# A long convolution by two-stage transforms: radix 64 first and radix 32 second, with real and imaginary parts on partitions

## The chip, the core and the metric

The kernel runs on one core of a Trainium2 chip. The metric is the time of one execution on the device, in microseconds (us). A core has a matrix engine (TensorE, written PE in the profile, with its weight loads listed apart as PEld), a vector engine (DVE), a scalar engine (ACT), a general engine (POOL, GpSimd) and a queue engine (SP) that mostly issues DMAs. TensorE reads its operands from SBUF and writes to PSUM; DVE and ACT read PSUM and write SBUF. A matmul may use only a part of the 128 x 128 array: the profile writes such a tile as rows x columns, so that 64*32 means 64 rows of contraction and 32 output partitions. Tiles in different places of the array can work at the same time.

## The reference

A layer norm feeds two branches, whose product is added to the input:

```python
xn = layernorm(x)                       # x: 2048 x 512
K  = einsum("dn,dnl,dn->dl", C, exp(dt*A*l), dt*B).real      # 512 x 2048 kernel, N = 128 states
y  = irfft(rfft(pad(xn.T)) * rfft(pad(K)))[:, :2048].T + xn * Dskip
g  = silu(gelu(xn @ w1 + b1) @ w2 + b2) # w1: 512 x 1792, w2: 1792 x 512
out = x + y * g
```

The convolution is causal, of length 2048, for each of 512 channels. The output must agree in float32.

## The kernel before

**Front.** A written order of steps (the string `ORDER`, lines 48 to 128) interleaves four kinds of work: the layer norm, the two dense products of the feed-forward branch (each value split into a high and a low part of type fp32r, so three products for one, lines 256 to 258 and 295 to 297), the parameters of the scan, and the generation of the kernel K (functions `gen_...`). K leaves for DRAM in `gen_keep` (line 666, tile `ko`). The kernel `K` for a group of channels comes from small matmuls of 128*32 with 64 columns of moving data (line 656).

**Scan.** The convolution is a product of length-2048 transforms with shifted frequencies (k + 1/4), so that no padding is needed. Channels are worked in four blocks `b` of 128 channels. A transform is done in two stages, 2048 = 32 x 64 before the change:

- `first_dft` (line 856) does the radix-32 stage for the signal (`u` = 0) and for the kernel (`u` = 1). The data of a block are the stationary operand, the small table `fc` is the moving one: 32*128 tiles, four row groups, 64 moving columns. `first_out` copies PSUM to the tile `X`, on ACT, and for block 0 on ACT and DVE.
- `second_dft` (line 874) does the radix-64 stage with twiddles folded into the table `mc`: 64*64 tiles, 128 moving columns, and real and imaginary parts added up in PSUM (the loop over `c`). There are eight groups `g` of frequencies in a block.
- `spectrum` (copy of the signal's spectrum by ACT, `uh`), `product` (two DVE products per group, tiles `t`) and `combine` (DVE, tile `Y`, four instructions of 64 partitions for two groups) multiply the two spectra.
- `back_dft` (line 914) is the first inverse stage: one full 128*128 matmul for a frequency, 128 moving columns; `back_out` copies to `Z`.
- `swing` transposes `Z` on TensorE, `swing_out` copies to `bs`, `last_dft` (line 969) does the last stage in 64*32 tiles with 512 moving columns (for part of the last block `rows_out`, line 1006, in 128*64 tiles), and `last_out` multiplies by the gate and adds the input (`gb`, `xb`), after which `store` writes to DRAM.

**Order.** In both parts the instructions of an engine run in the order of the program text; a framework adds the semaphore waits. `slot(b, g)` (line 1020) is one step of the scan: the second stage of group `g` of block `b`, beside it the first stage of block `b+1`, and the inverse stages of the same or the block before. After the front come four `first_dft` calls of block 0, mixed with the last products of the feed-forward branch (line 1105), and then 32 slots and a tail (lines 1125 to 1144).

**PSUM and DMA.** `bank` (line 804) gives out the one-bank PSUM tiles of the scan in turn from two tags of two; the second stage has its own two-bank tiles (`ri`, two of them). DMA issues of the scan wait in the queue of SP in program order: tables (`mc`, `tcn`), the raw signal (`raw`, from `xs`), the kernel (`in`, from `kgd`), gate and input for the tail (`gb`, `xb`), and the stores. `dsk` holds the skip weights, added to tap zero of the kernel by POOL in `side_skip` (line 851); it is filled in the front (`skip_load`, line 729).

All matmuls of the scan are of type float32, and the profile lists two weight loads and two matmuls for each call of such a matmul: for example 1,024 calls of line 883 (32 in each of 32 slots) stand as 2,048 in the profile. A transpose (line 936) stands as one.

Of the kernel before, what the change touches and what calls it, by code (L numbers as in the profile page):

```python
# [20 lines left out]
P = 128  # L21
# [4 lines left out]
N1, N2 = 32, 64  # L26
NB = 4
# [103 lines left out]
def _shape_constants():  # L131
    n1 = np.arange(N1)[:, None]
    k1 = np.arange(N1)[None, :]
    a = 2 * np.pi * n1 * (k1 + 0.25) / N1
    cf = np.tile(np.stack([np.cos(a), -np.sin(a)], 1), (G, 1, 1))
    cg = np.zeros((2, N1, 2, 3, N1))
    for hh in range(2):
        for c, v in enumerate((np.cos(a).T, -np.sin(a).T)):
            cg[hh, :, c, 0] = v
            cg[hh, :, c, 1:].reshape(N1, N1, 2)[:, :, hh] = v  # L140
    cg = cg.reshape(P, 3 * N1)
    n2 = np.arange(N2)[:, None]
    k2 = np.arange(N2)[None, :]
    cm = np.zeros((2, N2, N1, 3, N2))
    ct = np.zeros((2, N2, N1, 2, N2))
    for k in range(N1):
        th = 2 * np.pi * (n2 * (k + 0.25) / L + n2 * k2 / N2)
        c, s = np.cos(th), np.sin(th)
        cm[:, :, k, 0, :] = c
        cm[:, :, k, 1, :] = s  # L150
        cm[:, :, k, 2, :] = -s
        ct[0, :, k, 0, :] = c.T / L
        ct[1, :, k, 0, :] = -s.T / L
        ct[0, :, k, 1, :] = s.T / L
        ct[1, :, k, 1, :] = c.T / L
    ct = ct.reshape(P, N1, 2, 2, 2, 16).transpose(0, 1, 4, 5, 3, 2)
# [6 lines left out]
    return {  # L163
        "cf": cf.reshape(P, 2 * N1).astype(f),
        "cg": cg.astype(f),
        "cm": cm.reshape(P, N1 * 3 * N2).astype(f),
        "ct": ct.reshape(P, N1 * P).astype(f),
        "cb": cb.reshape(CH * NPC, CH * NPH).astype(ml_dtypes.bfloat16),
    }
# [3 lines left out]
def kernel(  # L173
# [7 lines left out]
    x_t = u[0].rearrange("(n h j t a q) d -> t h a j n q d", n=N1, h=2, j=2, t=2, a=2)  # L181
    o_l = out[0].rearrange("(r j q) d -> j r q d", j=2, q=NQ)
    o_t = out[0].rearrange("(n h j t a q) d -> t h a j n q d", n=N1, h=2, j=2, t=2, a=2)
# [20 lines left out]
    dsk = keep.tile([P, NB, DB], F32, name="dsk")  # L204
    GP.memset(dsk, 0.0)
    b1s = keep.tile([P, NF], F32, name="b1s")
    fc = keep.tile([P, 2 * N1], F32, name="fc")
# [452 lines left out]
    def gen_out(s):  # L660
        gen[s]["ko"] = ko = par.tile([P, DD, N2], F32, tag="ko", name=f"ko{s}", bufs=2)
        A.copy(ko, gen[s]["p"])

    def gen_keep(s):
        b, j = divmod(s, SPB)
        SY.dma_start(kgd[b][:, j * DD * N2:(j + 1) * DD * N2], gen.pop(s)["ko"].rearrange("p a b -> p (a b)"))
# [62 lines left out]
    def skip_load():  # L729
        for g in range(G):  # L730
            SY.dma_start(dsk[g * N1:g * N1 + 1], dskip.rearrange("(o b g d) -> g o b d", o=1, b=NB, g=G)[g])
        SY.dma_start(fc, cf)
# [50 lines left out]
    def open_front():  # L783
        SB["pf"] = pf = opened(p2, "pf", "right")
        SB["mc"] = pf.tile([P, N1, 3, N2], F32, name="mc")
        SB["psa"] = opened(p2, "psa", "right", bufs=2, space=PSUM)

    def open_mid():
        SB["pm"] = pm = opened(p2, "pm", "right")
        SB["ps"] = opened(pz, "psm", "left", bufs=2, space=PSUM)  # L790
        SB["tcn"] = pm.tile([P, N1, P], F32, name="tcn")
        SB["gc"] = pm.tile([P, N1], F32, name="gc")

    def table_load(t, src):
        w = t.shape[2] if len(t.shape) == 3 else t.shape[2] * t.shape[3]
        for k in range(0, N1, 8):
            d = t[:, k:k + 8]
            SY.dma_start(d.rearrange("p k m -> p (k m)") if len(t.shape) == 3 else d.rearrange("p k a m -> p (k a m)"),
                         src[:, k * w:(k + 8) * w])
# [13 lines left out]
    def stage_close():  # L813
        sg.close()
        SB["raw1"] = opened(fa, "raw", "left").tile([P, N2, DB], F32, name="raw1")

    def side_piece(b, g):
        t = side.setdefault(b, SB.get("raw1"))
        SY.dma_start(t[g * N1:(g + 1) * N1], xs.rearrange("(n m) (b g d) -> b g n m d", n=N1, b=NB, g=G)[b, g])

    def side_load(b):
        if b:
            t = SB["pf"].tile([P, N2, DB], F32, tag="in", name=f"raw{b}", bufs=2)
        else:
            t = wka.tile([P, N2, DB], F32, tag="xh", name="raw0", bufs=2)
# [4 lines left out]
    def side_turn(b):  # L830
        if b:
            t = SB["pf"].tile([P, DB, N2], F32, tag="in", name=f"in0_{b}", bufs=2)
        else:
            t = wka.tile([P, DB, N2], F32, tag="xl", name="in0_0", bufs=2)
        raw = side[b].rearrange("p m d -> p d m")
        side[b] = [[t[:, :DB // 2], t[:, DB // 2:]]]
        for h in range(2):
            d, r = side[b][0][h], raw[:, h * DB // 2:(h + 1) * DB // 2]
            GP.tensor_copy(d, r) if b else A.copy(d, r)

    def kernel_load(b):
        if b:
            k = SB["pf"].tile([P, DB, N2], F32, tag="in", name=f"in1_{b}", bufs=2)
            k = [k[:, :DB // 2], k[:, DB // 2:]]
        else:
            k = [wka.tile([P, DB // 2, N2], F32, tag="x", name=f"in1_0_{h}", bufs=2) for h in range(2)]
        for h in range(2):
            SY.dma_start(k[h], kgd[b].rearrange("p (h d m) -> p h d m", h=2, m=N2)[:, h])
        side[b].append(k)

    def side_skip(b):
        for h in range(2):
            k0 = side[b][1][h][:, :, 0]
            GP.tensor_add(k0, k0, dsk[:, b, h * DB // 2:(h + 1) * DB // 2])

    def first_dft(b, u, h, gs):
        if b not in xf:
            xf[b] = SB["pf" if b % 2 == 0 else "pm"].tile([P, 2, 2, N1, N2], F32, tag=f"X{b % 2}", name=f"X{b}")
        src = side[b][u][h]
        ps = [bank(f"s1_{b}_{u}_{h}_{g}").rearrange("p e (i m) -> p (e i) m", m=N2) for g in gs]  # L860
        for i in range(8):
            for g, p in zip(gs, ps):
                r = slice(g * N1, (g + 1) * N1)
                PE.matmul(p[:, i, :], src[r, 2 * i:2 * i + 2, :], fc[r], start=True, stop=True, skip_group_check=True)  # L864
        fp[b, u, h] = list(zip(gs, ps))

    def first_out(b, u, h, engs=(A, A, A, A)):
        for n, (g, p) in enumerate(fp.pop((b, u, h))):
            d, p = xf[b][:, :, u, :, 16 * g + 8 * h:16 * g + 8 * h + 8], p.rearrange("p i (c k) -> p c k i", c=2)
            A.copy(d, p) if engs[n] is A else engs[n].tensor_copy(d, p)  # L870
# [3 lines left out]
    def second_dft(b, g):  # L874
        mc = SB["mc"]
        p = SB["ps"].tile([P, 2, 2, 2, 2, N2], F32, tag="ri", name=f"s2_{b}_{g}", bufs=2)
        for jj in range(2):
            for o in range(2):
                for c in range(2):
                    for ka in range(2):  # L880
                        for r in range(2):
                            k, h = 4 * g + 2 * jj + ka, slice(r * 64, (r + 1) * 64)
                            PE.matmul(p[ka * 64:(ka + 1) * 64, r, o, :, jj], mc[h, k, ((0, 2), (1, 0))[c][o], :],  # L883
                                      xf[b][h, c, :, k, :], start=(c == 0), stop=(c == 1), skip_group_check=True)
        sp[b, g] = p

    def spectrum(b, g):
# [4 lines left out]
        if g % 2 == 0:  # L892
            sm[b, g // 2] = [pm.tile([P, 2, 2, 4, N2], F32, tag=f"t{i}", name=f"t{i}_{b}_{g}", bufs=2) for i in range(2)]
# [8 lines left out]
    def combine(b, j, c, eng, js=slice(0, 4)):  # L902
        t, w = sm[b, j]
        if (b, j) not in yy:
            yy[b, j] = SB["pm"].tile([P, 4, 2, P], F32, tag="Y", name=f"Y_{b}_{j}", bufs=2)
        Y = yy[b, j].rearrange("p j a (r x) -> p a r j x", r=2)
        for ka in range(2):
            r = slice(ka * 64, ka * 64 + 64)
            if c == 0:
                eng.tensor_sub(Y[0:64, ka, :, js], t[r, 0, :, js], w[r, 1, :, js])  # L910
            else:
                eng.tensor_add(Y[64:128, ka, :, js], t[r, 1, :, js], w[r, 0, :, js])

    def back_dft(b, j, h):
        Y = yy[b, j].rearrange("p j a m -> p (j a) m")
        p = bank(f"sa{b}_{j}_{h}")
        for e in range(4):
            PE.matmul(p[:, e, :], Y[:, 4 * h + e, :], SB["tcn"][:, 8 * j + 4 * h + e, :], start=True, stop=True)  # L918
        yy[b, j, h] = p

    def back_out(b, j, h, engs=(A,)):
        if (b, "Z") not in yy:
            yy[b, "Z"] = SB["pm"].tile([P, 32, 2, N1, 2], F32, tag="Z", name=f"Z{b}", bufs=2)
        k = 8 * j + 4 * h
        src = yy.pop((b, j, h)).rearrange("p k (x h c) -> p x h k c", h=2, c=2)
        dst = yy[b, "Z"][:, :, :, k:k + 4, :]
        w = 4 // len(engs)
        for i, eng in enumerate(engs):
            n = slice(w * i, w * i + w)
            eng.copy(dst[:, :, :, n], src[:, :, :, n]) if eng is A else eng.tensor_copy(dst[:, :, :, n], src[:, :, :, n])  # L930

    def swing(b, q4, jj, wide=None):
# [242 lines left out]
```

## Time and profile before

| what | value |
|---|---|
| three runs | 565.67, 566.75 and 886.81 us, median 566.75 us |
| profiled execution, first to last instruction (span) | 564.4 us |
| TensorE matmuls | 7,179 instructions, busy 543.8 us (96%) |
| DVE, ACT, POOL busy | 457.0, 411.5, 297.6 us |
| first `first_dft` in full | 395.39 us |
| first slot | 411.22 us |
| last matmul ends | about 557.3 us |

The page lists no time of its own for the profiled execution beside its span; the span is 2.35 us below the median of the runs, and 1.3 us below the fastest of them. All sums are made against the span. The busy time of TensorE counts a stretch in which any matmul is in flight, so two tiles at work together count once. A line of a timeline gives the start, the length, the engine, the line of the program, and how many instructions of one kind follow each other (x64); in square brackets stands how long the engine stood idle before it and what ended the wait. "issue" there means that nothing the profile shows was waited for.

### The profile page before, as it was taken

The numbers are of one execution on the slowest core, as the hardware profiler recorded it, in microseconds if no ns is written. First come the engines' busy times: TensorE is split into PE (matmuls) and PEld (weight loads), VectorE is DVE, ScalarE is ACT, GpSimd is POOL, SyncE is SP. The second block draws the span as 40 slices with busy tenths as digits, with TensorE's granted clock in tenths as the row PEclk, the third lists the DMA queues.
The fourth block names the chain that finished last, engine by engine and source line by source line (L and its number), as shares of the span: only waits on it lengthen the run. The fifth ranks groups of instructions, "written<-read, shape, count | busy, mean of one in ns | idle before, by whom it ended". The sixth has DMA issues, their size and how long they took to land.

```text
span 564.4 us, 17131 instructions
## 1 busy us (share of the span) xinstructions
PE 543.8 (96%) x7179; PEld 434.5 (77%) x7179; DVE 457.0 (81%) x699; ACT 411.5 (73%) x605; POOL 297.6 (53%) x403
## 2 busy tenths in 40 slices
PE   8898999999999999999999999999999999999995
PEld 8666777777777777777777777777779998988873
DVE  6999999999899789998897976886357656867874
ACT  3587998799977998777998787897355565564542
POOL 4648378449976679969743684370320305114323
PEclk9999999999999999999999999999999999999998
DMA  8967636845192364752258138313978583625945
GB/s 188 281 193 207 186 93 201 240 141 195 54 337 74 107 193 136 257 149 58 44 186 236 52 92 107 110 38 126 362 292 78 132 135 83 174 68 126 207 109 112
DMA packets 108344, 86.91 MB, mean 154 GB/s; under 512 B 44294, under 2 KB 87562, under 8 KB 108268
## 3 DMA queue, kind: packets, MB, share of 16 engines
q1 hardware_dynamic: 97584, 65.37, 44.3%
q0 software_dynamic: 9568, 19.93, 12.0%
q8 instruction: 56, 0.92, 0.7%
q10 hardware_dynamic: 1116, 0.53, 0.4%
q14 instruction: 20, 0.16, 0.1%
HBM read 52.25 MB, written 33.55 MB: 152 GB/s over the span
## 4 chain that ended last, share of the span: by engine, by line
PE 60%; DVE 17%; issue 8%; DMA 7%; ACT 3%; SPq 3%; POOL 2%; POOLq 0%; DVEq 0%; ACTq 0%
PE z L295 8%; PE z L296 7%; PE z L297 7%; PE f L256 7%; PE f L258 7%; PE f L257 6%; PE kg L656 5%; PE s L883 4%; PE s L864 3%; PE ph L595 2%; PE sa L918 2%; DVE ra L609 2%; DVE hl L282 2%; DMA xb<-in_A_u_dram 2%; DMA gb<-gd 1%
## 5 line engine op out<-in xcount | busy, mean ns | idle before, releaser
L618 POOL TENSOR_TENSOR mm<-mm,rc 128x32 f32<-128x32 f32 (+4 forms) x150 | 115.8, 772 | 11.8
L295 PE MATMUL z<-w2h,hh 128*128 128x512 f32 x224 | 97.9, 437 | 0.0
L256 PE MATMUL f<-xh,w1h 128*128 128x512 f32 x220 | 91.4, 415 | 0.1
L297 PE MATMUL z<-w2h,hl 128*128 128x512 f32 x224 | 88.5, 395 | 0.3 <-DVE hl L282 0.3
L296 PE MATMUL z<-w2l,hh 128*128 128x512 f32 x224 | 88.6, 395 | 0.0
L258 PE MATMUL f<-xh,w1l 128*128 128x512 f32 x220 | 87.0, 395 | 1.5 <-DVE w1l L241 1.5
L257 PE MATMUL f<-xl,w1h 128*128 128x512 f32 x220 | 86.7, 394 | 0.0
L883 PE MATMUL s<-X,mc 64*64 64x128 f32 x2048 | 63.8, 272 | 1.4 <-issue 1.4
L900 DVE TENSOR_TENSOR t<-s,uh 128x512 f32<-128x512 f32 x64 | 41.0, 685 | 26.6 <-ACT uh L891 26.3
L883 PEld LDWEIGHTS s<-X,mc 64*64 64x64 f32 x2048 | 56.1, 133 | 5.6 <-issue 3.3
L615 POOL COPY mm<-rc 128x32 f32<-128x32 f32 x30 | 14.1, 469 | 81.5 <-DVE e L648 48.9
L282 DVE TENSOR_TENSOR hl<-hf,hh 128x512 fp32r<-128x512 f32 x56 | 49.9, 894 | 5.6 <-ACT hh L276 5.6
L609 DVE SCALAR_TENSOR_TENSOR ra<-ra,ph 128x512 f32<-128x512 f32 x64 | 43.6, 681 | 8.9 <-ACT ra L603 7.9
L258 PEld LDWEIGHTS f<-xh,w1l 128*128 128x128 f32 x220 | 41.3, 188 | 12.3 <-DVE w1l L241 2.4
L270 ACT ACTIVATE hf<-f,b1s 128x512 f32<-128x512 f32 x56 | 38.2, 688 | 17.1 <-DVE hl L282 9.8
L297 PEld LDWEIGHTS z<-w2h,hl 128*128 128x128 f32 x224 | 42.1, 188 | 11.1 <-DVE hl L282 1.2
L295 PEld LDWEIGHTS z<-w2h,hh 128*128 128x128 f32 x224 | 42.5, 190 | 10.5 <-issue 1.0
L256 PEld LDWEIGHTS f<-xh,w1h 128*128 128x128 f32 x220 | 41.5, 189 | 9.8 <-ACT w1h L239 0.3
L296 PEld LDWEIGHTS z<-w2l,hh 128*128 128x128 f32 x224 | 42.3, 189 | 8.2 <-DVE w2l L241 0.2
L257 PEld LDWEIGHTS f<-xl,w1h 128*128 128x128 f32 x220 | 41.4, 188 | 9.0
L641 DVE TENSOR_TENSOR e<-mm,ra 128x1024 f32<-128x1024 f32 x32 | 42.9, 1340 | 5.8 <-ACT ra L629 3.3
L870 ACT COPY X<-s 128x512 f32<-128x512 f32 x56 | 28.9, 598 | 25.3 <-PE s L864 20.2
(185 smaller groups left out, 1163.6 us busy)
## 6 DMA issues: line engine op xcount, KB each, us to landing
x<-in_A_u_dram SPq DMA_DIRECT2D x16, 256.0 KB
xs<-x SPq DMA_DIRECT2D x16, 256.0 KB
xt_h<-xh POOLq DMA_DIRECT2D x4, 1024.0 KB, 5.4
xt_l<-xl POOLq DMA_DIRECT2D x4, 1024.0 KB, 7.4
kgd<-ko SPq DMA_DIRECT2D x32, 128.0 KB
za<-zo SPq DMA_DIRECT2D x4, 1024.0 KB
xh<-xt_h POOLq DMA_DIRECT2D x4, 1024.0 KB, 6.7
xl<-xt_l POOLq DMA_DIRECT2D x4, 1024.0 KB, 10.1
```

The source lines that it names most:

```text
L256: PE.matmul(p, wh[:, k, :], xh[:, k, :], start=(k == 0), stop=False)
L257: PE.matmul(p, wh[:, k, :], xl[:, k, :], start=False, stop=False)
L258: PE.matmul(p, wl[:, k, :], xh[:, k, :], start=False, stop=(k == KD - 1))
L282: V.tensor_sub(hl, hf, hh)
L295: PE.matmul(z, hh[:, s], wh, start=(f0 == 0 and not rows), stop=False)
L296: PE.matmul(z, hh[:, s], wl, start=False, stop=False)
L297: PE.matmul(z, hl[:, s], wh, start=False, stop=(f0 == FA - 1))
L609: V.scalar_tensor_tensor(ra[:, 0, c], ra[:, 1, c], MAGIC, p, op0=ALU.subtract, op1=ALU.subtract)
L618: GP.tensor_mul(mv[:, :, 0:3:2, w:2 * w], mv[:, :, 0:3:2, 0:w], rc[:, 2 + 2 * i:4 + 2 * i, :].rearrange("p j c -> p c j").unsqueeze(3).to_ ...
L641: V.tensor_mul(e1, m1.unsqueeze(1).to_broadcast([P, 2, CH, N1]), ra[:, :, :, :N1])
L883: PE.matmul(p[ka * 64:(ka + 1) * 64, r, o, :, jj], mc[h, k, ((0, 2), (1, 0))[c][o], :], xf[b][h, c, :, k, :], start=(c == 0), stop=(c == 1 ...
L900: V.tensor_mul(t, p[:, i, :, 1].unsqueeze(1).to_broadcast([P, 2, 2, P]), uh)
```

## The change

The two radices change places: 2048 = 64 x 32 forward, the radix-64 stage first. The tables change with them, and the loops are cut so that a matmul of the three transform stages uses one of eight tiles of the array.

- `first_dft`: 64 rows of contraction, 32 output partitions (64*32), 64 moving columns; the four column groups are real and imaginary part of two channels, the two row groups are two halves of the channels. A block is worked in eight calls of 64 matmuls instead of four calls of 32. The real and the imaginary part of `X` now lie on partitions beside each other.
- `second_dft`: one matmul with 64 rows (real and imaginary part together) replaces two that were added up in PSUM; 32 output partitions, 128 moving columns, 32 matmuls in a slot as before.
- `combine`: two DVE instructions of 128 partitions for two groups instead of four of 64.
- `back_dft`: 32 rows, 64 output partitions, 64 moving columns, two matmuls added up for each result, 128 matmuls in a call and two calls for a block, instead of 32 full matmuls for a block. It fills four banks at once. `back_out` copies two banks on ACT and two on DVE.
- `last_dft`: two 128*64 matmuls with 512 columns for a quarter block, instead of eight 64*32 for half a block; `rows_out` is gone, since all quarters now leave as rows.
- `slot` gets a new order, the same for all blocks; `gen_out` and `gen_keep` write K in two halves; `side_piece` reads 256 bytes at a time instead of 128; `kernel_load` issues eight DMAs instead of two; `mc` and `tcn` shrink (3.1 to 2.1 MB, 2.1 to 1.0 MB); `dsk` moves into the scan's own pool, and is filled after the front; the tag `in` has three buffers instead of two; `Y` has three.

```diff
-    def first_dft(b, u, h, gs):
+    def first_dft(b, i):
+        u, h, n = i // 4, i // 2 % 2, i % 2
...
-        ps = [bank(f"s1_{b}_{u}_{h}_{g}").rearrange("p e (i m) -> p (e i) m", m=N2) for g in gs]
-        for i in range(8):
-            for g, p in zip(gs, ps):
-                r = slice(g * N1, (g + 1) * N1)
-                PE.matmul(p[:, i, :], src[r, 2 * i:2 * i + 2, :], fc[r], start=True, stop=True, skip_group_check=True)
+        ps = [bank(f"s1_{b}_{i}_{e}").rearrange("p a (c k) -> p (a c) k", k=M1) for e in range(2)]
+        for x in range(8):
+            for rc in range(4):
+                for e in range(2):
+                    rows, q = slice(e * M1, (e + 1) * M1), slice(rc * 32, (rc + 1) * 32)
+                    PE.matmul(ps[e][q, x, :], src[rows, 16 * n + 2 * x + rc // 2, :], fc[rows, rc % 2, :],
+                              start=True, stop=True, skip_group_check=True)
...
     def second_dft(b, g):
...
         for jj in range(2):
             for o in range(2):
-                for c in range(2):
-                    for ka in range(2):
-                        for r in range(2):
-                            k, h = 4 * g + 2 * jj + ka, slice(r * 64, (r + 1) * 64)
-                            PE.matmul(p[ka * 64:(ka + 1) * 64, r, o, :, jj], mc[h, k, ((0, 2), (1, 0))[c][o], :],
-                                      xf[b][h, c, :, k, :], start=(c == 0), stop=(c == 1), skip_group_check=True)
+                for q in range(4):
+                    for r in range(2):
+                        k, h = 8 * g + 4 * jj + q, slice(r * 64, (r + 1) * 64)
+                        PE.matmul(p[q * 32:(q + 1) * 32, r, o, :, jj], mc[h, k, o, :], xf[b][h, :, k, :],
+                                  start=True, stop=True, skip_group_check=True)
...
-    def combine(b, j, c, eng, js=slice(0, 4)):
+    def combine(b, j, eng, js=slice(0, 4)):
...
+        eng.tensor_sub(Y[:, 0, :, js], t[:, 0, :, js], w[:, 1, :, js])
+        eng.tensor_add(Y[:, 1, :, js], t[:, 1, :, js], w[:, 0, :, js])
...
-        for e in range(4):
-            PE.matmul(p[:, e, :], Y[:, 4 * h + e, :], SB["tcn"][:, 8 * j + 4 * h + e, :], start=True, stop=True)
+    def back_dft(b, lo, hi):
+        ps = [bank(f"sa{b}_{lo}_{q}").rearrange("p a (j m) -> p (a j) m", m=2 * M2) for q in range(4)]
+        for j in range(lo, hi):
+            Y = yy[b, j // 4]
+            for c in range(2):
+                for q in range(4):
+                    for r in range(2):
+                        k, m = slice(q * 32, (q + 1) * 32), slice(r * 64, (r + 1) * 64)
+                        PE.matmul(ps[q][m, j - lo, :], Y[k, j % 4, c, m], SB["tcn"][k, j, c, :],
+                                  start=(c == 0), stop=(c == 1), skip_group_check=True)
...
     def last_dft(b, t):
-        py = [bank(f"y{b}_{t}_{h}") for h in range(2)]
-        for a in range(2):
+        py = bank(f"y{b}_{t}")
+        for jj in range(2):
+            PE.matmul(py[64 * jj:64 * jj + 64], SB["gc"], yy[b, t, "s"][:, jj], start=True, stop=True, skip_group_check=True)
...
+    def slot(b, g):
...
+        if b and g in (3, 4, 6, 7):
+            last_dft(b - 1, (3, 4, 6, 7).index(g))
+        if b and g == 1:
+            back_dft(b - 1, 8, 16)
+        if g == 5:
+            back_dft(b, 0, 8)
+        sw = (2, 3, 4, 6).index(g) if b and g in (2, 3, 4, 6) else None
+        if sw is not None:
             for jj in range(2):
+                swing(b - 1, sw, jj)
+        second_dft(b, g)
+        if nxt:
+            first_dft(b + 1, g)
+        if b and g == 1:
+            back_out(b - 1, 8, 16, (A, V, A, V))
+        if g == 5:
+            back_out(b, 0, 8, (A, V, A, V))
...
+        SB["dsk"] = dsk = pf.tile([P, NB, HB], F32, name="dsk")
+        GP.memset(dsk, 0.0)
+        for e in range(2):
+            SY.dma_start(dsk[e * M1:e * M1 + 1], dskip.rearrange("(o b e d) -> e o b d", o=1, b=NB, e=2)[e])
```

More of the change, by code (lines that the diff above doesn't have):

```diff
@@ new lines, in wide_bank @@
+    def wide_bank(b, t):
+        return SB["ps"].tile([P, 2, 4, P], F32, tag="ri", name=f"w{b}_{t}", bufs=2)
+    def slot(b, g):
+        nxt, last = b + 1 < NB, b == NB - 1
+        if last and g == 0:
+            big = SB["pf"].tile([P, 2, 32, P], F32, tag="X0", name="last")
+            for t in range(4):
+                gx[b, t, "t"] = (big[:, 0, 4 * t:4 * t + 4], big[:, 1, 4 * t:4 * t + 4])
+        if b and g in (3, 4, 6, 7):
[6 more added lines that the diff above has]
+        if sw is not None:
+            for jj in range(2):
+                swing(b - 1, sw, jj)
[6 more added lines that the diff above has]
+            back_out(b, 0, 8, (A, V, A, V))
+        if sw is not None:
+            for jj in range(2):
+                swing_out(b - 1, sw, jj, A)
+        spectrum(b, g)
+        if nxt:
+            first_out(b + 1, g)
+        if b and g in (3, 4, 6, 7):
+            last_out(b - 1, (3, 4, 6, 7).index(g))
+        product(b, g)
+        if g % 2:
+            combine(b, g // 2, V)
+        if b and g in (0, 1, 2, 5):
+            tail_load(b - 1, (0, 1, 2, 5).index(g))
```

365 lines of the change are left out of this document (126 added, 239 removed).

## The prediction

> **What bounds the kernel now.** First the page's shares, then the scan by stretches, then the timeline of TensorE.
>
> ```profile
> span 564.4 us, 17131 instructions
> PE 543.8 (96%) x7179; PEld 434.5 (77%) x7179; DVE 457.0 (81%) x699; ACT 411.5 (73%) x605; POOL 297.6 (53%) x403
> q8 instruction: 56, 0.92, 0.7%
> ```
>
> ```profile
> 395.30:557.30 162.00, 157.15 (x3599) 136.82 (x3599) 107.32 (x162) 85.78 (x155) 43.65 (x50) 1.00 0.64 157
> 440.00:500.00 60.00, 60.00 (x1496) 54.53 (x1488) 40.86 (x60) 35.66 (x66) 12.98 (x12) 1.00 0.60 135
> ```
>
> Columns are busy us and instructions of PE, PEld, DVE, ACT and POOL, then granted clock, DMA share and GB/s. From the first full `first_dft` to the last matmul are 162.0 us, and in 60 us amid the slots PE is busy throughout at full clock, with DVE at 68% and ACT at 59%. The matmuls set the pace, so their groups come next:
>
> ```profile
> L883 PE MATMUL s<-X,mc 64*64 64x128 f32 x2048 | 63.8, 272 | 1.4 <-issue 1.4
> L656 PE MATMUL kg<-e,e 128*32 128x64 f32 x2048 | 35.2, 220 | 0.0
> L864 PE MATMUL s<-fc,in 32*128 32x64 f32 x1024 | 33.8, 273 | 1.1 <-ACT X L870 1.1
> L918 PE MATMUL sa<-tcn,Y 128*128 128x128 f32 x256 | 33.4, 282 | 1.8 <-DVE Y L910 1.8
> L975 PE MATMUL y<-bs,gc 64*32 64x512 f32 x112 | 8.8, 601 | 0.0
> ```
>
> One wait here belongs to no engine: 1.4 us of "issue" before L883. The timeline of PE shows it:
>
> ```profile
> 413.52 0.44 PE L883 MATMUL s<-X,mc 64*64 64x128 f32 x6 [0.34 <-issue]
> 413.89 2.01 PE L864 MATMUL s<-fc,in 32*128 32x64 f32 x64
> 415.84 1.96 PE L883 MATMUL s<-X,mc 64*64 64x128 f32 x58
> 418.72 2.19 PE L883 MATMUL s<-X,mc 64*64 64x128 f32 x70 [0.93 <-issue]
> ...
> 430.52 1.32 PE L883 MATMUL s<-X,mc 64*64 64x128 f32 x39
> 432.00 0.97 PE L883 MATMUL s<-X,mc 64*64 64x128 f32 x25 [0.17 <-issue]
> ```
>
> PE stops in the midst of a run of 64 matmuls, with no one to wait for, and between two stops stand 6 + 64 + 58 = 128 matmuls, each with its weight load (a pair). The q8 row explains the number: 0.92 MB in 56 packets is 16.4 KB a packet, and 0.92 MB over the 2 x 7,179 instructions of TensorE is 64 bytes each, so a packet carries 256 instructions, **128 pairs**. It is TensorE's program, and PE stood because the next packet was not there. The DMA view of four stretches, each with its instruction row if it has one, tells when the packets went:
>
> ```profile
> q1 hardware_dynamic: 348, 1.12, 101.1%
> q1 hardware_dynamic: 128, 0.14, 35.0%
> q8 instruction: 1, 0.02, 6.1%
> q0 software_dynamic: 116, 0.36, 84.3%
> q8 instruction: 1, 0.02, 5.7%
> ```
>
> The first row is 413.5 to 416.3 us: other queues fill the 16 engines and no instruction packet moves. The second and third are 416.3 to 417.4: the packet. PE resumes at 418.72, 2.4 us after the packet began. The fourth is 418.7 to 420.0, again without one, and the fifth 420.0 to 421.1, the next packet. So the following packet is asked for only when PE has entered the one before it: 1.3 us to its start, 2.4 us from there to use. **A turn is 1.3 + 2.4 = 3.7 us for 128 pairs**, and was 418.72 - 413.52 = 5.2 us while tables were loading. Today this mostly hides: at L883's 63.8 / 2,048 = 31 ns a pair, 128 pairs take 4.0 us.
>
> **The change, part by part.** *Work in the array.* How long does one pass take with eight tiles? The timeline of PE shows two shapes at work, and the chain of waits (start, us, what) the segments of a slot and the last block's L1009:
>
> ```profile
> 465.72 1.09 PE L975 MATMUL y<-bs,gc 64*32 64x512 f32 x16
> 466.74 2.05 PE L918 MATMUL sa<-tcn,Y 128*128 128x128 f32 x16
> ...
> 392.76 1.10 PE L656 MATMUL kg<-e,e 128*32 128x64 f32 x64
> 393.80 0.50 PE L295 MATMUL z<-w2h,hh 128*128 128x512 f32 x1
> ```
>
> ```profile
> 422.85 1.91 PE s L883 x64
> 424.76 1.98 PE sa L918 x16
> 426.74 1.91 PE s L883 x64
> 428.65 1.94 PE s L864 x64
> ...
> 555.91 1.06 PE y L1009 x4
> ```
>
> L975 has eight tiles at once: 16 matmuls of 512 columns in 466.74 - 465.72 = 1.02 us, two passes. L656 (four tiles, 64 columns) does 64 in 393.80 - 392.76 = 1.04 us, 16 passes of 0.06. L883 (four tiles, 128 columns) does 16 passes in 1.91: 0.11 each, and 0.17 for the change of tile shape. If eight tiles overlap as four do:
> - `second_dft`: 64 in 8 passes of 0.11 + 0.17 for the change of shape = 1.05 against 1.91; 32 slots: -27.5 us.
> - `first_dft`: 128 in 16 passes of 0.06 + 0.15 = 1.05, eight times a block instead of 1.94 four times: 33.6 against 31.0: +2.6 us.
> - `back_dft`: 256 in 32 passes of 0.06 + 0.1 = 2.0, twice a block, against four of 1.98 (x16): -15.8 us.
> - `last_dft`: 16 of 1.06 (the L1009 row) against seven of 1.02 and two of 1.06: +7.7 us.
>
> Sum **-33 us** in the array. The transposes stay.
>
> *Instructions.* By calls, two pairs each: `first_dft` 2,048 calls instead of 512, so 1,024 pairs become 4,096; `second_dft` stays at 2,048; `back_dft` 1,024 calls instead of 128, 256 pairs become 2,048; the last stage 120 become 64. Added: 3,072 + 1,792 - 56 = **4,808 pairs**, 37.6 packets. The window from 395.3 to 557.3 holds 3,599 today; it will hold 8,407, or **65.7 packets**, and 128 pairs take 0.9 us (first, back) to 1.9 us (second) of array time. Less than a turn, everywhere: PE will wait at nearly every packet boundary.
>
> The price of a turn is not seen in a sustained run, so it is bounded: 2.4 us (no delay to the start) and 5.2 us (the loaded turn). I take 3.6, beside the 3.7 that the rows give, since that start had another queue at 84% next to it. Three turns at the start, under the table loads, take 5.2. Sum: 65.7 x 3.6 + 3 x 1.6 = 241.3 us against 162.0: **+79 us**. The ends: 65.7 x 2.4 = 158 (-4 us) and 65.7 x 5.2 = 342 (+180 us). The array's gain of 33 us is then no gain at all, being inside the waits.
>
> [...]
>
> *Other edits, at nothing.* They hide behind PE, which now waits more:
>
> ```profile
> L910 DVE TENSOR_TENSOR Y<-t,t 64x512 f32<-64x512 f32 x30 | 20.6, 685 | 0.7
> L912 DVE TENSOR_TENSOR Y<-t,t 64x512 f32<-64x512 f32 x30 | 24.0, 799 | 0.7
> L930 ACT COPY Z<-sa 128x512 f32<-128x512 f32 x31 | 18.2, 586 | 16.9 <-PE sa L918 16.9
> L854 POOL TENSOR_TENSOR in<-in,dsk 128x16 f32<-128x16 f32 x8 | 2.0, 249 | 37.5 <-DMA in<-kgd 37.5
> ```
>
> `combine` halves, -22 us of DVE; 16 of the `Z` copies move to DVE, +11; and ACT has 9 less (16 x 586 ns); both engines have 30% and more free in the window above, and without PE's cover both would still have less to do than today. Tables load 2 MB less. `kernel_load` adds 24 DMA issues on SP, the tails drop more (three loads and two stores a quarter instead of six and four). The new `dsk` memset (POOL) and its two DMAs stand in SP's queue ahead of `mc` and behind the release of the front's memory; SP would hold back `mc`, wanted by the first slot, and the kernel, wanted by the third of four first-stage calls. The first-stage calls now take eight packets, some 35 us instead of 16, which covers it; without cover a us or two. The larger `kgd` piece count costs at most the same. The tail after the last matmul keeps its 7 us.
>
> **The rivals.**
> - *The program arrives in time* (chance 0.10). Then the array sets the pace: 564.4 - 33 = 531, about **533 us**, faster. It decides at a turn below 162.0 / 65.7 = 2.47 us on average, and holds wholly below about 1.8, the array time of 128 pairs of the second stage. For it: the 60 us without an idle moment. Against: they need only 12 packets, one in 5 us, and the way from a packet's start to its use is 2.4 us already.
> - *A turn of just 2.4 us* (0.04): 562 us, within 2%.
> - *Eight tiles with 64 columns run no faster than four* (0.04): the change would not do what it says. Then 8,192 pairs at 1.04 / 64 = 16.3 ns are 133 us against 61.1 + 31.0 + 31.7 = 123.8, with `last_dft` +17 us, **584 us**. L975 speaks against it, but at 512 columns. [...]
>
> **How the numbers follow.** The likeliest is the packet-bound scan, 0.82: span 564.4 + 79.3 = 643.7, and 2.35 us more to the median as before (566.75 - 564.4), **646 us**. The average turn could be 2.9 us (a start delay half of the one seen) to 4.3 (every second or third one loaded): 65.7 x 2.9 = 191 gives +33 with the loaded turns, 600 us; 65.7 x 4.3 = 283 gives +125, 692 us. That range leaves out the two cases at the bottom, the 584 of the third, and a little at each end: 0.2 in all. Faster by over 2% 0.10, within 2% 0.04, slower 0.86; 2% is about what a measurement of this kernel can tell from no change.
>
> **What would show it.** In the changed profile: some 93 or 94 packets in the q8 row and 11,987 matmuls; idle time of PE put down to "issue", in stops every 128 pairs, with 3.4 to 3.8 us from one resumption to the next; bursts of eight matmuls of 64 columns in about 0.06 us; DVE's `Y` group near 22 us; the clock perhaps below 1.00, since PE works only a third of the time, which a turn still covers at half speed. Wrong would be a scan with PE busy all through, packets less than 2.4 us apart, or waits at semaphores (`Z`, `X`, the four banks of `back_dft`) longer than a turn, which would add to it.

## The result and the profile after

The changed kernel takes **695.26 us** (median of four runs, 689.54 to 696.67) against 566.21 us before (one of its four runs, a disturbed one of 886.81 us, is left out of the comparison). The ratio is 1.2238, with a 95% interval from 1.2148 to 1.2328: 22% slower. The prediction was 646 us with a range of 600 to 692, so the direction and most of the loss were foreseen, but the measured time lies 3 us above the range.

From the page of the changed kernel; the two rows of digits are slices of a fortieth of the span, with the busy tenths of TensorE and the granted clock in tenths:

```profile
span 694.4 us, 26653 instructions
...
PE 579.8 (83%) x11987; PEld 448.7 (65%) x11987; DVE 441.5 (64%) x678; ACT 405.0 (58%) x589; POOL 294.9 (42%) x397
...
PE   7889999999999999999999865555586767774876
...
PEclk9999999999999999999999989776577858675778
...
q8 instruction: 94, 1.54, 1.0%
```

There are 11,987 matmuls and 94 packets of program, exactly the forecast's counts. Up to the scan little has changed (it begins 1.5 us earlier); in the scan TensorE is busy 50 to 80% instead of throughout, and its clock falls. The scan by stretches (busy us and instructions of PE, PEld, DVE, ACT, POOL, then granted clock, DMA share, GB/s), the first row from the first `first_dft` to the last matmul, the second over 64 whole turns of the program:

```profile
393.80:687.30 293.50, 194.00 (x8405) 152.29 (x8405) 91.08 (x140) 79.03 (x139) 41.57 (x44) 0.74 0.36 82
395.50:676.00 280.50, 182.03 (x8169) 144.03 (x8169) 87.02 (x134) 74.58 (x131) 39.12 (x42) 0.74 0.36 83
```

Before, the same work took 162.0 us with PE busy 157.15 at a clock of 1.00. Now it takes 293.5 us, of which PE has nothing in flight for 99.5. DVE and ACT are busy less than a third of the time, so neither sets the pace. What PE waited for (total us, number of waits, longest):

```profile
PE s L860 <- issue: 51.4, 27, 5.1
PE sa L915 <- issue: 31.9, 15, 4.8
PE s L880 <- issue: 8.2, 9, 2.0
PE s L880 <- ACT X L868: 3.5, 3, 1.2
PE sa L915 <- ACT X L868: 2.2, 8, 0.4
```

91.5 us stand before the three stages of small tiles as "issue", with nobody to wait for; the largest wait for another engine is 3.5 us. The timeline of PE shows the program arriving in blocks:

```profile
566.06 2.25 PE L915 MATMUL sa<-tcn,Y 32*64 32x64 f32 x128 [1.33 <-issue]
569.53 1.47 PE L915 MATMUL sa<-tcn,Y 32*64 32x64 f32 x70 [1.22 <-issue]
570.93 2.50 PE L880 MATMUL s<-X,mc 64*32 64x128 f32 x61
573.02 0.45 PE L860 MATMUL s<-fc,in 64*32 64x64 f32 x10
573.22 0.43 PE L880 MATMUL s<-X,mc 64*32 64x128 f32 x3
573.24 2.02 PE L860 MATMUL s<-fc,in 64*32 64x64 f32 x112
576.75 0.31 PE L860 MATMUL s<-fc,in 64*32 64x64 f32 x6 [1.49 <-issue]
```

PE resumes at 566.06, does exactly 128 pairs and stops; it resumes at 569.53 and does 70 + 61 + 10 + 3 + 112 = 256, two packets, before the next stop. The turns last 3.47 us, and 7.22 us for two. The DMA view of 567.1 to 568.4 has the packet for 569.53:

```profile
q8 instruction: 1, 0.02, 4.9%
```

In the stretch before it, 566.1 to 567.1, no instruction packet moves. So the packet starts only after PE has entered the one before; by the records of the 64 turns each does, 0.03 to 5.89 us after. For this one, 1.1 us pass to its start, 1.0 us for the packet itself and 1.3 us more to its first use, close to the 1.3 and 2.4 us read off before the change.

### The profile page after: what moved, and what is told of

Its sections match the earlier page's. It is cut to its first block, busy times and chain, and to the rows that moved or that the text cites. A ratio compares the mean times of both kernels' runs of the same rounds, so it can differ in the third digit from the quotient of the medians.

```text
span 694.4 us, 26653 instructions
## 1 busy us (share of the span) xinstructions
PE 579.8 (83%) x11987; PEld 448.7 (65%) x11987; DVE 441.5 (64%) x678; ACT 405.0 (58%) x589; POOL 294.9 (42%) x397
## 3 DMA queue, kind: packets, MB, share of 16 engines
q8 instruction: 94, 1.54, 1.0%
## 5 line engine op out<-in xcount | busy, mean ns | idle before, releaser
L860 PE MATMUL s<-fc,in 64*32 64x64 f32 x4096 | 63.2, 253 | 51.4 <-issue 51.4
L860 PEld LDWEIGHTS s<-fc,in 64*32 64x32 f32 x4096 | 54.7, 119 | 59.4 <-issue 59.0
L971 POOL TENSOR_TENSOR xb<-gb,xb 128x512 f32<-128x512 f32 x12 | 15.3, 1276 | 178.9 <-DVE gb L970 178.9
L868 ACT COPY X<-s 128x512 f32<-128x512 f32 x56 | 30.5, 588 | 93.1 <-PE s L860 85.9
L915 PE MATMUL sa<-tcn,Y 32*64 32x64 f32 x2048 | 39.8, 295 | 35.8 <-issue 31.9
L880 PE MATMUL s<-X,mc 64*32 64x128 f32 x2048 | 53.2, 336 | 11.9 <-issue 8.2
L915 PEld LDWEIGHTS sa<-tcn,Y 32*64 32x64 f32 x2048 | 33.7, 181 | 41.9 <-issue 35.4
L926 DVE COPY Z<-sa 128x512 f32<-128x512 f32 x16 | 10.3, 686 | 76.5 <-PE sa L915 76.5
L880 PEld LDWEIGHTS s<-X,mc 64*32 64x32 f32 x2048 | 38.6, 128 | 22.2 <-issue 16.4
```

The source lines that it names most:

```text
L860: PE.matmul(ps[e][q, x, :], src[rows, 16 * n + 2 * x + rc // 2, :], fc[rows, rc % 2, :], start=True, stop=True, skip_group_check=True)
L880: PE.matmul(p[q * 32:(q + 1) * 32, r, o, :, jj], mc[h, k, o, :], xf[b][h, :, k, :], start=True, stop=True, skip_group_check=True)
L915: PE.matmul(ps[q][m, j - lo, :], Y[k, j % 4, c, m], SB["tcn"][k, j, c, :], start=(c == 0), stop=(c == 1), skip_group_check=True)
```

## The experiments

Nine kernels, each built from the kernel before or the changed one. A table first; "window" is a stretch of the scan that holds whole turns, and clock and DMA share are those of that window.

| kernel | time, us | ratio to before (95% interval) | packets | window, us, and its packets | clock | DMA share |
|---|---|---|---|---|---|---|
| before | 566 to 567 | 1 | 56 | 162.0, 28 | 1.00 | 0.64 |
| changed | 695.3 | 1.224 (1.215 to 1.233) | 94 | 280.5, 64 | 0.74 | 0.36 |
| first stage in 64*64 tiles | 635.3 | 1.121 (1.109 to 1.132) | 78 | 216.5, 48 | 0.81 | 0.46 |
| inverse stage in 32*128 tiles | 672.1 | 1.185 (1.177 to 1.194) | 86 | 256.5, 57 | 0.80 | 0.40 |
| both wide variants | 607.9 | 1.074 (1.066 to 1.081) | 70 | 189.5, 41 | 0.90 | 0.53 |
| before, second stage cut | 612.0 | 1.079 (1.072 to 1.087) | 72 | 197.5, 43 | 0.93 | 0.48 |
| before, first stage cut | 595.6 | 1.048 (1.040 to 1.056) | 64 | 180.5, 35 | 0.92 | 0.55 |
| before, first stage cut, slots evened | 592.8 | 1.043 (1.036 to 1.050) | 62 | 178.5, 34 | 0.93 | 0.55 |
| changed, array work added | 721.3 | 1.271 (1.261 to 1.281) | 95 | 304.5, 65 | 0.85 | 0.34 |
| changed, DMA traffic added | 732.8 | 1.291 (1.281 to 1.301) | 94 | 317.5, 64 | 0.72 | 0.60 |
| changed, DMA traffic removed | 671.7 | 1.183 (1.173 to 1.194) | 94 | 253.5, 64 | 0.78 | 0.17 |

### Fewer pairs for the same passes: the first stage

```diff
-            for rc in range(4):
+            for c in range(2):
...
-                    rows, q = slice(e * M1, (e + 1) * M1), slice(rc * 32, (rc + 1) * 32)
-                    PE.matmul(ps[e][q, x, :], src[rows, 16 * n + 2 * x + rc // 2, :], fc[rows, rc % 2, :],
+                    rows, q = slice(e * M1, (e + 1) * M1), slice(c * 64, (c + 1) * 64)
+                    PE.matmul(ps[e][q, x, :], src[rows, 16 * n + 2 * x:16 * n + 2 * x + 2, :], fc[rows, c, :],
```

> The changed kernel, but the first stage loads two channels at once as weights (64*64 tiles, four at a time, instead of 64*32, eight at a time): 32 calls where there were 64, and as many passes of 64 columns as before. The order of the parts of X on the partitions is then another one, so the spectra are not those of the reference; the work of every other instruction is the same. Theory (the program of TensorE arrives too slowly): 2,048 pairs or 16 packets fewer at 4.0 to 4.4 us each, 64 to 70 us less than 695, so 620 to 635. Rival (the array is slow because its clock is held at about 0.74 in the scan): the same passes, so 685 to 700. Rival (waits for PSUM copies): the same copies, 685 to 700.

635.3 us, at the theory's upper edge, and both rivals (685 to 700) are out. The window of 48 turns:

```profile
395.50:612.00 216.50, 157.90 (x6270) 123.47 (x6264) 88.49 (x134) 74.54 (x131) 40.03 (x42) 0.81 0.46 108
```

The same products in half the instructions save 60 us for 16 packets, 3.75 us each. The busy time of PE in the scan falls as well, 182.0 to 157.9 us, though the passes in the array are as many. Not all of the 60 us need be packets: where no stop falls into it, a call of 64 wide pairs takes 1.09 us at full clock (472.28 to 473.37 in the kernel with both wide variants) and one of 128 narrow pairs 1.46 us (516.74 to 518.20 in the kernel with added work). Over 32 calls that is up to 12 us of array work, which this run doesn't separate.

### Fewer pairs for the same passes: the inverse stage

```diff
-                    for r in range(2):
-                        k, m = slice(q * 32, (q + 1) * 32), slice(r * 64, (r + 1) * 64)
-                        PE.matmul(ps[q][m, j - lo, :], Y[k, j % 4, c, m], SB["tcn"][k, j, c, :],
+                    k = slice(q * 32, (q + 1) * 32)
+                    PE.matmul(ps[q][:, j - lo, :], Y[k, j % 4, c, :], SB["tcn"][k, j, c, :],
```

> The changed kernel, but the backward stage takes both halves r in one matmul (32*128 tiles, 128 weight columns) instead of two of 32*64: 64 calls where there were 128, same results. Each pass is now held by loading 128 weight columns, 0.11 us instead of 0.06, so the array has 14 us more to do at full clock. Theory (program): 1,024 pairs or 8 packets fewer at 4.0 to 4.4 us, 32 to 35 us less, 658 to 665. Rival (slow array): 14 to 20 us more, 709 to 715. Rival (PSUM copies): unchanged, 690 to 700.

672.1 us: 23 us saved by 8 packets, 2.9 us each. That is less than the theory's 30 to 37 and far from the rival, which had a loss. Its 0.11 and 0.06 us a pass are estimates from L864 and L656 before: with 64 moving columns and four tiles at a time, 64 pairs of 128 weight columns take 1.94 us there and 64 of 32 weight columns 1.04. Of 64 weight columns they take 1.09 us (446.75 to 447.84 in the kernel with evened slots). A weight load takes 186 ns on average with 128 columns (L864 before) and 133 ns with 64 (L883).

### Both together

```diff
-            for rc in range(4):
+            for c in range(2):
...
-                    for r in range(2):
-                        k, m = slice(q * 32, (q + 1) * 32), slice(r * 64, (r + 1) * 64)
+                    k = slice(q * 32, (q + 1) * 32)
```

> The changed kernel with both wide variants together: the first stage in 64*64 tiles (half the calls) and the first inverse stage in 32*128 tiles (half the calls), the second stage as it is in 64*32 tiles. As in the first-stage variant alone, the parts of X lie in another order than the second stage reads them, so the result is not the reference's; the work is the same. 3,072 pairs less than the changed kernel, 24 packets: 70 packets in all. Theory (each packet of the scan costs its turn as long as TensorE waits for it): the two savings measured alone add up, 60 + 23 us, so 695.3 - 83.2 = 612 us, range 605 to 620. First rival (with 5,333 pairs in the scan TensorE waits at few boundaries, the saving of the last packets is lost in array work): 622 to 635. Second rival (the radices and the layout cost nothing, all of the loss is pairs, and 41.7 packets at the old kernel's 5.8 us or less hide): 560 to 580.

607.9 us. The two savings add up (60 + 23 = 83 expected, 87 measured), and the first rival falls, though PE now waits for only part of the packets. The second rival falls too: 70 packets are still 42 us slower than before. What PE waited for in this kernel:

```profile
PE s L880 <- issue: 14.8, 11, 2.7
PE s L860 <- issue: 9.6, 5, 3.7
...
PE sa L914 <- issue: 3.0, 2, 2.1
```

27.4 us of "issue" are left of 91.5.

### More pairs in the kernel before: the second stage

Each second-stage matmul of 128 columns becomes two of 64, for signal and kernel:

```diff
+                for u in range(2):
...
-                                      xf[b][h, c, :, k, :], start=(c == 0), stop=(c == 1), skip_group_check=True)
+                                          xf[b][h, c, u, k, :], start=(c == 0), stop=(c == 1), skip_group_check=True)
```

> The kernel before, with every matmul of its second stage cut into two of 64 columns (signal and kernel apart): 2,048 pairs more, the same columns, the same results. Theory (program): 5,647 pairs or 44 packets between 395 and the end, at 4.0 to 4.4 us make 176 to 194 us against 162 now, so 580 to 600, with stops at packet boundaries all through the scan. Rival (the array alone counts): twice the passes at half the length, no change, 564 to 570.

612.0 us, worse than the theory's range, and the rival that the columns alone count is out. Tiles, columns, layout and radices are the same; the instructions are more, and the array has hardly more to do: 128 cut pairs take 2.09 us at full clock against 1.98 for 64 uncut ones (442.63 in the kernel before), under 4 us in 32 slots.

```profile
452.97 2.09 PE L884 MATMUL s<-X,mc 64*64 64x64 f32 x128
```

What PE waited for, and the window of the scan:

```profile
PE s L884 <- issue: 17.7, 14, 2.7
PE s L864 <- issue: 10.5, 6, 4.3
```

```profile
396.50:594.00 197.50, 166.98 (x5538) 150.61 (x5531) 100.57 (x154) 82.30 (x148) 39.28 (x46) 0.93 0.48 125
```

So the old kernel, cut finer, gets the new one's signature: stops on "issue" in two stages (28.2 us) and a clock below 1. This isolates the cause: pairs, not radices. The kernels with both wide variants and with this cut, with 70 and 72 packets, take 607.9 and 612.0 us, though their radices differ.

### More pairs in the kernel before: the first stage

```diff
-                PE.matmul(p[:, i, :], src[r, 2 * i:2 * i + 2, :], fc[r], start=True, stop=True, skip_group_check=True)
+                for a in range(2):
+                    PE.matmul(p[a * 64:(a + 1) * 64, i, :], src[r, 2 * i + a, :], fc[r], start=True, stop=True, skip_group_check=True)
```

> The kernel before, with each matmul of its first stage cut into two of 64 weight columns (32*64 tiles, eight at a time): 1,024 pairs more, the same results. The passes, now held by loading 128 weight columns (0.11 us), should take 0.06, so the 31 us of the first stage become about 17. Theory (program): 36 packets at 4.0 us make 144 us, just below the array's 148, so 552 to 562, with more stops at packet boundaries than before. Rival (no limit from the program): 551 to 553. Rival (eight tiles run no faster than four): 566 or more.

595.6 us: the expectation was missed by more than 30 us, and on the wrong side. I had reasoned with the mean: 35 packets in the scan, over four us for each, should all hide. The timeline of PE shows why the mean is the wrong measure:

```profile
432.29 0.34 PE L865 MATMUL s<-fc,in 32*64 32x64 f32 x7 [1.65 <-issue]
432.56 3.27 PE L884 MATMUL s<-X,mc 64*64 64x128 f32 x64
...
443.21 0.69 PE L865 MATMUL s<-fc,in 32*64 32x64 f32 x25 [1.90 <-issue]
443.82 3.35 PE L884 MATMUL s<-X,mc 64*64 64x128 f32 x64
...
453.18 1.98 PE L884 MATMUL s<-X,mc 64*64 64x128 f32 x64
455.08 2.05 PE L919 MATMUL sa<-tcn,Y 128*128 128x128 f32 x16
...
458.97 1.62 PE L865 MATMUL s<-fc,in 32*64 32x64 f32 x128
460.52 0.67 PE L884 MATMUL s<-X,mc 64*64 64x128 f32 x16
```

In a pair of slots, 16 full matmuls take 2 us with 16 pairs and then the first stage takes 1.6 us with 128. In the 64 turns of the changed kernel no packet started before PE had entered the one before it. If one packet ahead is all there is here too, time won in the sparse stretch can't be saved up for the dense one, and PE stops there (1.65 us before 432.29, 1.90 before 443.21). And the stop is not all: 64 matmuls of L884 take 1.98 us at 453.18 and 3.27 to 3.35 shortly after a stop. The windows of two such groups, the slow one and the usual one, differ in the clock column, 0.58 against 1.00:

```profile
432.56:435.76 3.20, 3.20 (x68) 2.87 (x65) 0.28 (x1) 1.07 (x2) 0.00 (x0) 0.58 0.53 84
453.18:455.08 1.90, 1.90 (x69) 1.73 (x64) 0.18 (x1) 1.90 (x4) 1.68 (x1) 1.00 0.03 9
```

The gain in the array was also smaller than I had put it: 128 pairs of eight tiles take 458.97 to 460.52 = 1.55 us instead of 1.94. The time alone would fit the rival that eight tiles run no faster than four (566 or more); these 1.55 us speak against it.

### The same cut, with the slots evened out

First-stage work is spread so that each slot has half a call, together with one second stage and half an inverse stage, and blocks 1 to 3 alone are cut:

```diff
+        if nxt:
+            first_dft(b + 1, i // 2, i % 2, (0, 1) if g % 2 == 0 else (2, 3))
...
-            back_dft(*sa, 0)
-            back_dft(*sa, 1)
+            back_dft(*sa, sh)
```

> The kernel before with the first stage of blocks 1 to 3 cut in two as in e4 (768 pairs more), and the order of the slots evened out: half a first-stage call, one second-stage call, one backward call, and one transpose group or last-stage call in each slot, so that 128 pairs hold some 4.3 us of array work everywhere. Theory (program, and it is the dense stretches of e4 that cost): a turn of 3.8 us is covered, few stops, and the 11 us of passes saved stay saved: 552 to 562. Rival (each packet costs TensorE something whatever its density): six packets more, 567 to 590.

592.8 us: missed again, and not shown to be better than the uneven one (595.6, the intervals overlap). The timeline of PE tells why the experiment isn't clean:

```profile
446.75 1.16 PE L868 MATMUL s<-fc,in 32*64 32x64 f32 x64
447.84 1.98 PE L887 MATMUL s<-X,mc 64*64 64x128 f32 x64
...
499.29 1.02 PE L868 MATMUL s<-fc,in 32*64 32x64 f32 x27 [5.50 <-POOL in L839]
```

Half a call holds only two of the four row groups, hence four tiles at once instead of eight: 64 pairs take 447.84 - 446.75 = 1.09 us, two such calls 2.18 us, which is more than the uncut 1.94. It also has more changes of tile shape, and one wait of 5.5 us for POOL's copy into `in`. What PE waited for in it:

```profile
PE s L868 <- POOL in L839: 5.5, 1, 5.5
PE s L887 <- issue: 4.4, 6, 1.1
PE s L868 <- issue: 2.0, 3, 1.6
```

The stops on "issue" are small in both stages (in the uneven kernel 11.7 us stood before the first stage and 5.2 before the second). Some 7 of the 26 us that were lost lie ahead of the slots, in the first stage of block 0, which isn't cut here: from 399.87 to the first slot at 418.14 pass 18.3 us, where before it was 11.1 us (400.08 to 411.22). PE is busy throughout there, behind a stop of 1.38 us that waited for ACT, but at a granted clock of 0.50:

```profile
401.16:418.23 17.07, 17.07 (x193) 13.89 (x193) 5.94 (x9) 6.20 (x10) 4.47 (x5) 0.50 0.91 362
```

Whether an even density would hide all packets, or each packet costs something whatever its density, is therefore left open.

### Array work added to the changed kernel

Two full 128*128 matmuls of 512 columns ahead of each second stage, whose result is overwritten:

```diff
+        for _ in range(2):
+            PE.matmul(p[:, 0].rearrange("p o u a x -> p (o u a x)"), ident, mc[:, 0:8].rearrange("p k o x -> p (k o x)"),
+                      start=True, stop=True, skip_group_check=True)
```

> The changed kernel with two more full 128*128 matmuls of 512 columns ahead of the second stage of every slot, into a PSUM tile that the second stage overwrites: 128 pairs, one packet, but four passes of 0.43 us a slot, 55 us of array work at full clock. Theory (program): the array works while TensorE waits for its next packet, and it is idle less, so its clock stays higher: 685 to 710. Rival (slow array): 55 us or more on top, 745 to 780.

721.3 us, between the two: 26 us more for 32 x 1.88 = 60 us of work (the group below at full clock; 0.47 us a pass, where the estimate had 0.43). Neither side had it right. More than half is hidden in the waits, so the array isn't what limits the scan. Where the rest goes isn't shown by a run of its own. One packet more is part of it (95 for 94). By the trace, PE also took up some 24 packets more than 1.8 us after their end, against 10 in the changed kernel, so more blocks of 128 pairs lasted longer than the turn.

```profile
512.91 3.00 PE L876 MATMUL s<-mc,ident 128*128 128x512 f32 x4
...
516.74 1.53 PE L860 MATMUL s<-fc,in 64*32 64x64 f32 x128
518.20 0.98 PE L935 MATMUL w<-ident,Z 128*128 128x128 f32 x7
519.90 0.33 PE L935 MATMUL w<-ident,Z 128*128 128x128 f32 x1 [0.72 <-issue]
520.07 1.88 PE L876 MATMUL s<-mc,ident 128*128 128x512 f32 x4
```

At 512.91 the same four take 3.00 us, at a granted clock of 0.64 (1.00 at 520.07). In a filled slot, a stop is now short (0.72 us), and the clock of the window rises from 0.74 to 0.85.

### DMA traffic added, and removed

Added: in each slot SP issues two copies from DRAM to DRAM, 32 MB in all, which nothing waits for.

```diff
+        for i in range(2):
+            SY.dma_start(dup[2 * (8 * b + g) + i], u[0].rearrange("(n p a) d -> n p (a d)", p=P, a=2)[(2 * g + i) % 8])
```

> The changed kernel with two copies of 512 KB from DRAM to DRAM issued by SP in every slot, which nothing waits for: 32 MB more through the DMA engines, the work of every engine the same. Theory (packets of the program that start late stand behind other DMA traffic): more turns with a start over 2 us after TensorE has entered the packet before, the mean turn 0.5 to 1 us longer, 725 to 765. Rival (the late starts come from waits of TensorE itself): 688 to 700.

Removed: in the slots most loads fall away, and POOL fills the tiles with constants.

```diff
+        if b:
+            GP.memset(t, 0.0)
+            return
...
+            if b > 1:
+                GP.memset(k[h], 0.0)
+                continue
...
-        q.dma_start(gb, gd[b].rearrange("p (q m) -> p q m", m=P)[:, n])
...
+        GP.memset(gb, 1.0)
+        GP.memset(xb, 0.0)
```

> The changed kernel, but in the slots the signal and the kernel of blocks 2 and 3, the gates and the inputs of the tail aren't loaded: POOL fills their tiles with constants, and the signal of block 1 is still loaded in the front. The stores stay, and so does all work of TensorE, ACT and DVE; the output is not the reference's. Theory (late packets stand behind DMA traffic): the late starts in the slots go, 15 to 25 us less, 670 to 682. Rival: 688 to 700.

732.8 us with the copies, 671.7 us without the loads; both as the theory had it. The windows of the same 64 packets, with the copies and without the loads:

```profile
395.50:713.00 317.50, 182.55 (x8177) 144.62 (x8184) 87.02 (x134) 74.53 (x131) 38.98 (x42) 0.72 0.60 178
```

```profile
395.50:649.00 253.50, 175.60 (x8180) 140.05 (x8188) 87.00 (x134) 74.54 (x131) 54.03 (x68) 0.78 0.17 42
```

At a DMA share of 0.17, 0.36 and 0.60 the 64 packets take 253.5, 280.5 and 317.5 us: turns of 3.96, 4.38 and 4.96 us on average. The trace has a record of each instruction packet, and by these it is the start that moves: from PE's entry into a packet to the start of the next one pass 1.28, 1.61 and 2.38 us on average, and 4, 13 and 26 of the 64 start later than 2 us. The packet's own transfer stays at about 1.1 us.

## Why the prediction was right, and where its size was wrong

**Right: what bounds the scan.** The rows of the changed kernel have the counts (94 packets, 11,987 matmuls), the stops between multiples of 128 pairs, the quiet turn of 3.47 us and the hidden array work. That pairs set the time is shown from both sides: pairs added to the old kernel cost 45 us for 16 packets, of which under 4 us are array work; pairs taken away from the new one save 87 us for 24, of which up to 12 us may be array work of the first stage. In the finely cut old kernel, too, the packet boundaries don't hide: 28.2 us of "issue" and 45 us of time stand there, where blocks of 128 pairs are shorter than a turn.

**Right: the other edits cost nothing.** The `Y` group of DVE, forecast near 22 us, by shape:

```profile
L904 DVE TENSOR_TENSOR Y<-t,t 128x512 f32<-128x512 f32 x16 | 11.1, 693 | 0.6
L905 DVE TENSOR_TENSOR Y<-t,t 128x512 f32<-128x512 f32 x16 | 10.9, 684 | 0.0
```

It is 22.0. Waits for ACT's `X` come to 5.7 us, and 7.1 us pass after the last matmul, for the 7 forecast.

**Wrong: the price of a turn.** The step that failed is "I take 3.6 ... Three turns at the start, under the table loads, take 5.2", 241.3 us in all. The same term measures 293.5 us, 52 more, and that is the whole miss (the span is 694.4 against 643.7; the first stage begins 1.5 us earlier). By the runs:

- **27 us are DMA traffic** all along the slots (280.5 against 253.5 us without most of the loads). I had charged 4.8 us for it, in three turns. The loaded turn was in view, 5.2 us at 413.52, but I took it for a feature of the table loads, which end early. Other loads do the same: the starts at 2.9, 2.9 and 5.9 us after PE's entry at 489.33, 555.62 and 621.43 fall among loads of `raw`, `gb` and `xb`. Whether the stores do so isn't shown. Here is one with `in`, in the timeline of PE in the changed kernel and the DMA view of 404.7 to 408.8, the stretch after PE entered the packet that runs dry at 406.3:

```profile
403.82 2.44 PE L860 MATMUL s<-fc,in 64*32 64x64 f32 x203
411.36 1.09 PE L860 MATMUL s<-fc,in 64*32 64x64 f32 x53 [5.09 <-issue]
```

```profile
q1 hardware_dynamic: 411, 1.51, 96.5%
```

No instruction packet moves for some 4 us, with the 16 engines 96.5% taken by loads of `in`; PE stands for 5.09 us.

- **18 us lie in the turns even without that traffic** (253.5 against 64 x 3.6 + 4.8 = 235.2). The median turn in that run is 3.75 us, which makes 64 x 0.15 = 10 of it. The rest goes with late starts that remain and with blocks whose own work outlasts the turn, most of them at a granted clock of 0.50. The windows over the four matmuls of L964 in the changed kernel, at the low clock and at the full one, take 1.9 and 1.0 us; both stand shortly after a stop, of 0.80 and 0.84 us:

```profile
542.40:544.30 1.90, 1.90 (x7) 0.29 (x4) 0.56 (x1) 1.07 (x2) 0.00 (x0) 0.50 0.02 4
548.90:549.90 1.00, 1.00 (x12) 0.20 (x4) 0.00 (x0) 0.89 (x2) 0.00 (x0) 1.00 0.42 76
```

I had written that a turn still covers PE at half speed. It does for most blocks: in 55 of the 64 turns of the changed kernel PE takes up the packet within 1.8 us of its end, and so was waiting for it. It doesn't for all. How the 18 us divide is estimated, not measured by a run of its own.

- **7 us are the edges**, the first pairs and the tail of the window (13.0 us outside the 64 turns, where 1.7 packets at 3.6 were charged). No run divides these further.

The range ended at an average turn of 4.3 us; it was 4.38, and the edges came on top.

**Wrong, but without effect: the array.** I had put a first-stage call of 128 pairs at 1.05 us. It takes 1.46 us even with no stop in it (see below). Of the 33 us of array work that were to go, a part was never there; inside the waits it doesn't show. The rival "eight tiles run no faster than four" is not decided by the time of the changed kernel, since the array doesn't set it: 60 us of added work cost 26. The rate decides it: 128 pairs in 1.46 us are 11 ns a pair, where the rival had 16.3.

## What to carry to other kernels

Count TensorE's instructions as well as its passes: here a float32 call was four, and 1.54 MB of program for 23,974 of them came in 94 packets, 256 a packet; in the 64 turns of the scan each packet started after PE had entered the one before, 1.61 us on average. Where 128 pairs held less work than a turn, here 3.5 us undisturbed and 4.4 us on average, the fetch set the time. This has to be asked stretch by stretch (in the kernel with the first stage cut the mean should have covered every turn, and it was 4.8% slower than before), and at the DMA load of the same stretch. The change to eight small tiles brought a higher rate and more instructions together: 11 ns a pair for 16.3 (L656 before, four tiles), and 4,808 pairs more. Of two tilings with the same passes, the one with wider tiles won by 60 us here, most of it packets.

## What the runs showed of the hardware that was not expected

- **Data traffic delayed the program.** With the DMA share of the scan at 0.17, 0.36 and 0.60, the mean time from entering a packet to the start of the next was 1.28, 1.61 and 2.38 us. Where the request waits, the trace doesn't show.
- **The clock fell in long stretches.** In the changed kernel's trace the granted clock is 1.00 or 0.50, and the stretches at 0.50 last 3.4 to 30.7 us (the longest from 482.9 to 513.7); a figure between the two is a mean over both. Stops stand ahead of many of them: 2.51 us before 441.27, 2.28 before 461.17 and 2.29 before 481.68 for the stretches that begin at 441.97, 462.45 and 482.93. But not every stop brings one: in the kernel with evened slots the clock is 1.00 from 418.3 to 496.7, with stops of 1.56 us before 426.97 and 1.43 us before 459.95. And busy work doesn't end one at once, as the 17.07 us above show. What decides stays open. The scan as a whole ran at 0.74. Work that falls into a stretch at the low clock takes longer, 3.27 us instead of 1.98 for the 64 matmuls of L884 in the kernel with the first stage cut (0.58 and 1.00), and costs time where the next wait doesn't hide it.
- **Small tiles ran slower than forecast, and PE's busy time hid a short stop.** In the changed kernel 128 first-stage pairs, following other work without a stop that the timeline shows, take 1.84 us:

```profile
519.40 1.84 PE L860 MATMUL s<-fc,in 64*32 64x64 f32 x128
```

By the records of this burst, 0.22 us pass between the starts of its 26th and 27th pair. The matmuls in flight, 0.22 to 0.24 us long, cover it, so it counts as busy. It is a packet boundary: after the stop at 516.11 the timeline has 26 + 4 + 8 + 64 pairs before this burst, and 26 more make 128. In the kernel with added work the same 128 take 518.20 - 516.74 = 1.46 us, 11 ns a pair, where the forecast had 1.05 us and about 8. What sets this pace stays open.
